# Criss-cross window attention: TensorE queues VectorE's scores before their banks are free

## The chip, the cores and the metric

The kernel runs on one core of a Trainium2 chip. The metric is device time in microseconds. One execution was also profiled: for it there is a trace of every instruction on TensorE (PE), its weight loads (PEld), VectorE (DVE), ScalarE (ACT), GpSimd (POOL) and SyncE (SP).

## The reference

An image of 224 x 224 tokens with 96 channels is projected to queries, keys and values. The first 48 channels attend within horizontal stripes of 8 rows, the other 48 within vertical stripes of 8 columns; each stripe is a window of 1792 tokens, with 28 windows in each direction. Then comes an output projection.

```python
qkv = jnp.einsum('bhwc,cd->bhwd', x, wqkv)          # x (1, 224, 224, 96), wqkv (96, 288)
scale = C2 ** (-0.5)                                # C2 = 48
qh = q[..., :C2].reshape(B * nh, sw * W, C2)        # 28 windows of 1792 tokens
ah = _softmax(jnp.einsum('bqc,bkc->bqk', qh, kh) * scale, axis=-1)
oh = jnp.einsum('bqk,bkc->bqc', ah, vh).reshape(B, H, W, C2)
...                                                 # the same over vertical stripes: ov
return jnp.einsum('bhwc,cd->bhwd', o, wo)           # o = concat(oh, ov)
```

## The kernel before

Two windows are worked at a time, so there are 28 pairs P (14 horizontal, then 14 vertical). For a pair, the scores are cut into 49 groups: for each 512 queries (the last chunk has 256) a group is 128 keys (256 keys in the last chunk) of both windows. A group G is a tile of 128 x 1024 scores in two PSUM banks; there are 28 x 49 = 1372 of them. Each has to be exponentiated and then multiplied with V (`plan_PV`, L829), which adds up in one of the banks 6 and 7 until a chunk's groups are all done. The row sums come from a column of ones in V, and the division is in the output projection.

Exponentials are the bulk of the work, and three engines share them:

- ScalarE ("a" tiles): one activation from PSUM to a buffer `PTA` (L892). Its scores go in turn to banks 0 and 1 and to banks 2 and 3. `qA` lists the tiles whose scores are queued, `actA` those whose exponential is.
- VectorE ("d" tiles): an approximation by a polynomial and the bits of the float, four passes over the 1024 columns (L911, L913, L915, L916), the last into `PTD`. The scores go to banks 4 and 5, `dps` (L898).
- GpSimd ("p" tiles): VectorE copies the scores from the same banks 4 and 5 to SBUF (L1033), and GpSimd makes six passes over them (L983 to L992), the last into `PTP`.

Scores for the last two kinds are made with one more row of the operands (KD = 50 against KA = 49), so in the trace a matmul of L198 or L724 with 50 rows is for banks 4 and 5, one with 49 rows for ScalarE.

Banks 4 and 5 hold one tile at a time. `D["cur"]` is that tile; `D["free"]` is the event after which the banks may be written again, the last pass (L916) or the copy (L1033).

The order of every engine's instructions is fixed when the program is built, by a small planner that is part of the kernel. It keeps a clock `now`, and for each engine the time at which it is free (`tfree`). `add` (L175) puts an instruction at the end of an engine's list, with a duration from the source, and gives back an event: a semaphore, its value and `vis(e)`, the planned time at which the others can see it. When an engine is free, its `pick_` function chooses what comes next; if it chooses nothing, the clock goes on to the next alarm. Afterwards `emit` (L1209) writes the lists out: an instruction whose event hasn't come waits on the semaphore, and everything behind it on its engine waits too.

`pick_pe` (L741) chooses for TensorE, in this order:

1. scores for ScalarE, when their two banks have been released by the exponential before last; else it notes in `nextfree` when that will be;
2. scores for a "p" tile, if banks 4 and 5 have none in work, fewer than NZP = 2 "p" tiles are out, and the scores fit before `nextfree`;
3. scores for a "d" tile, under the same condition on the banks;
4. one PV tile, if GRP tiles are ready (or as many as the chunk has left), or NBA - UTH of the NBA = 8 `PTA` buffers are in use, or a burst is under way and no projection is wanted;
5. a projection ("fill"): Q, K, V of the next pair or the output projection of the one before. They use the bank of 6 and 7 that PV doesn't.

If it finds nothing, `keep_warm` (L1135) may add a matmul that changes no result.

`fits` (L769) is the test of time: the work, plus 100 ns where TensorE changes between the array split in 64 x 64 tiles ("r64", for scores) and the undivided one ("r128"), may end up to `slack` ns after `nextfree`. The slack is SLACK = 160 for PV and projections, DSLACK for scores into banks 4 and 5. In planned ns, scores take 240, a PV tile 235, a pass of VectorE 1142, an exponential 917.

DUEO is read in L1120 alone, in the branch for `ORD == 0`; ORD is 1 (L90).

Of the kernel before, what the change touches and what calls it, by code (L numbers as in the profile page):

```python
# [22 lines left out]
def bass_standalone__window_attn_cswin__vision_kernel(  # L23
# [32 lines left out]
    NZP = 2  # L56
# [5 lines left out]
    SLACK = 160  # L62
    PACE = 0.5
    FDUE = 20
    DSLACK = 120
    GRP = 3
    NBA = 8
    LOOK = 7
    NPT = 400
# [5 lines left out]
    KWL = 0  # L75
    HOLD = 110
    HOLD2 = 0
    DUEO = 18
    DUES = 2.5
    DUE1 = 5  # L80
    DUEV = 20
    LATE = 10
    UTH = 2
    PSPAN = 20
    SAFE = 100
    WGAP = 170
    PADA = 5
    PADB = 1
    ENDD = 2
# [17 lines left out]
    with es:  # L107
# [60 lines left out]
        def vis(e):  # L168
            return e[2] if e is not None else 0.0
# [138 lines left out]
        def pv_bank(chg):  # L308

            if chg in pvb:  # L310
                return pvb[chg]
            return min((6, 7), key=lambda i: 1e18 if bank_free[i] == "busy" else vis(bank_free[i]))
# [368 lines left out]
        def progress():  # L681
            while lowest[0] < NGTOT and taken[lowest[0]] is not None:
                lowest[0] += 1
            return lowest[0]

        def tile_deps(G):
            P, g = divmod(G, NG)
            c = GROUPS[g][0]
            step = 512 if P == 0 else PCH
            kts = GROUPS[g][1]  # L690
            need = [(q_ready, i) for i in range((CH_Q0[c] + CH_SIZES[c] - 1) // step + 1)]
            need += [(k_ready, i) for i in range(kts[0] * 128 // step, (kts[-1] * 128 + 127) // step + 1)]
            if any((P, i) not in r for r, i in need):
                return None
            return [r[(P, i)] for r, i in need]

        def plan_QK(G, base, kk, waits):
            P, g = divmod(G, NG)
            c, kts = GROUPS[g]
            q0, qs = CH_Q0[c], CH_SIZES[c]  # L700
            b = P % 2


            def tiles(i):
                return [(64 * wdw, 64 * kh, wdw, kh) for wdw in range(2) for kh in range(2)]

            def k_ap(kt, r0, kh):
                return KT_sb[b][r0:r0 + kk, kt * 128 + 64 * kh:kt * 128 + 64 * kh + 64]

            def fn_w(e):  # L710
                for r0, c0, wdw, kh in tiles(0):
                    ins = load_weights(e, k_ap(kts[0], r0, kh), (r0, c0))
                return ins

            def fn(e):
                ins = None
                for i, kt in enumerate(kts):
                    for r0, c0, wdw, kh in tiles(i):
                        o = bank(base + wdw)[64 * kh:64 * kh + 64, i * qs:(i + 1) * qs]
                        rhs = QT_sb[b][r0:r0 + kk, q0:q0 + qs]  # L720
                        if i == 0:
                            ins = loaded_matmul(e, o, k_ap(kt, r0, kh), rhs, (r0, c0))
                        else:
                            ins = e.matmul(o, lhsT=k_ap(kt, r0, kh), rhs=rhs, start=True, stop=True)  # L724
                return ins
            ops["pe"].append((tile_deps(G), fn_w, False))
            return add("pe", waits, fn, 240.0, 425.0, "r64")
# [6 lines left out]
        D = dict(n=0, cur=None, np=0)  # L734
        P_out = []
# [5 lines left out]
        def pick_pe():  # L741
            t = now[0]

            m = len(qA)
            nextfree = None
            if progress() < NGTOT:
                G = progress()
                deps = tile_deps(G)
                if deps is not None:
                    ws = list(deps)  # L750
                    ok = True
                    if m >= 2:
                        if len(actA) <= m - 2:
                            ok = False
                        else:
                            ws.append(actA[m - 2])
                    if ok:
                        tv = max(vis(w) for w in ws)
                        if tv <= t:
                            taken[G] = "a"  # L760
                            lastA[0] = G
                            ev = plan_QK(G, 2 * (m % 2), KA, ws)
                            qA.append((G, ev))
                            return True
                        nextfree = tv

            pe_next[0] = nextfree

            def fits(occ, mode="r128", slack=SLACK):  # L769
                if mode != pe_mode[0]:  # L770
                    occ += SWITCH
                if mode != "r64":
                    occ += SWITCH
                return nextfree is None or t + occ <= nextfree + slack or nextfree - t > 1500.0

            if D["cur"] is None and len(P_out) < NZP and D["np"] < NPT and fits(240.0, "r64", DSLACK):
                lo = max(progress(), lastA[0]) + LOOKP
                for G in range(lo, min(lo + PSPAN, NGTOT - 10)):
                    deps = tile_deps(G) if taken[G] is None else None
                    ws = list(deps) + [D.get("free")] if deps is not None else [None]  # L780
                    if deps is not None and all(vis(w) <= t for w in ws):
                        taken[G] = "p"
                        D["np"] += 1
                        P_out.append(G)
                        zi = D["np"] % NZP
                        ev = plan_QK(G, 4, KD, ws)
                        D["cur"] = dict(G=G, k=0, prev=ev, qk=ev, p=zi)
                        return True
            if D["cur"] is None and fits(240.0, "r64", DSLACK):
                G = max(progress(), lastA[0]) + LOOK  # L790
                while G < NGTOT and taken[G] is not None:
                    G += 1
                if G < NGTOT - ENDD:
                    deps = tile_deps(G)
                    if deps is not None:
                        ws = list(deps) + [D.get("free")]
                        if all(vis(w) <= t for w in ws):
                            taken[G] = "d"
                            ev = plan_QK(G, 4, KD, ws)
                            D["cur"] = dict(G=G, k=0, prev=ev, qk=ev)  # L800
                            return True

            ready = []
            chg = pv_cur[0]
            if chg < NCHT:
                bi = pv_bank(chg)
                P = chg // NCH
                if (not pv_first[chg] or (bank_free[bi] != "busy" and vis(bank_free[bi]) <= t)) and P in v_ready and vis(v_ready[P]) <= t:
                    ready = [G for G in pv_left[chg] if G in pt_ev and vis(pt_ev[G][0]) <= t]
            used = sum(b is not None for b in bufA)  # L810
            f = next_fill()
            nleft = len(pv_left[chg]) if chg < NCHT else 0

            want_fill = f is not None and fits(f.occ) and not (nleft <= NRES and chg + 1 < NCHT and progress() < f.due + RDUE)
            late = want_fill and progress() > f.due - LATE and used < NBA - 1
            if ready and fits(235.0) and not late and (len(ready) >= min(GRP, nleft) or used >= NBA - UTH or not want_fill and inburst[0] > 0):
                for G in ready[:1]:
                    plan_PV(chg, G)
                inburst[0] = len(ready) - 1
                return True  # L820
            inburst[0] = 0
            if want_fill:
                f.start()
                fills_todo.remove(f)
                evac_q.append(f)
                return True
            return False
# [48 lines left out]
        def next_fill():  # L876
            for f in fills_todo:
                if f.target <= progress() and f.ready():
                    return f
            return None  # L880
# [198 lines left out]
        def early_qk(G):  # L1079
# [7 lines left out]
            qA.append((G, plan_QK(G, 2 * (G % 2), KA, tile_deps(G) + [actA[G - 2]])))  # L1087
        pad(PADA)
        early_qk(2)
# [20 lines left out]
        def refill():  # L1110

            while NXT["P"] < NP and progress() >= NXT["P"] * NG:
                P = NXT["P"]
                NXT["P"] += 1
                if P + 1 < NP:
                    pf = prep_fills(P + 1)
                    order = pf["K"] + pf["Q"][:2] + pf["V"] + pf["Q"][2:] if ORD == 0 else pf["K"] + pf["Q"] + pf["V"]
                    for i, f in enumerate(order):
                        f.target = P * NG + PACE * i
                        f.due = P * NG + NG - LOOK - DUEO + DUES * i if ORD == 0 else P * NG + (DUES * i + DUE1 if i < 8 else NG - DUEV + DUES * (i - 8))  # L1120
                        fills_todo.append(f)
# [13 lines left out]
        def keep_warm():  # L1135
# [5 lines left out]
            if tail[0] or 3000.0 - busy < WARM or t - tfree["pe"] < 60.0:  # L1141
                return False
            if pe_next[0] is not None and pe_next[0] - t < WGAP:
                return False
# [131 lines left out]
```

The softmax here doesn't subtract the row's maximum and nothing guards it: scores larger than these inputs give would overflow.

## Time and profile before

| | |
|---|---|
| time, median of 4 runs | 1082.83 us (1082.6 to 1083.24) |
| the profiled execution | 1082.6 us |
| its span, first to last instruction | 1080.8 us |
| granted TensorE clock | 0.998 |
| tiles by ScalarE, VectorE, GpSimd | 1161, 117, 94 |
| four passes of VectorE, mean of one | 1.22, 1.22, 1.21, 1.21 us |
| copy of VectorE for GpSimd, mean | 1.22 us |
| six passes of GpSimd, mean of one | 1.04, 1.89, 1.04, 2.13, 2.13, 1.05 us |

The counts are those of the lines L892, L911 and L1033 in the profile. A record of ScalarE or VectorE runs until its result is written, and overlaps the beginning of the next, so the distance from one start to the next is shorter than the mean shown. In rows of the trace, "<-" before a line names what ended the idle time of an engine.

### The profile page before, as it was taken

Reading aid. Unit: us, or ns where it says so; the run is one execution under the profiler, and the core shown is the slowest. Engines: PE = TensorE matmul, PEld = TensorE weight load, DVE = VectorE, ACT = ScalarE, POOL = GpSimd, SP = SyncE. Lnnn points to the kernel's source line nnn. Section 1 sums busy time; section 2 is a strip of 40 time slices with the busy share of each in tenths; the row PEclk is TensorE's granted clock in tenths of the full one; section 3 lists DMA queues with packets and bytes.
Section 4 is the critical chain, followed back from the end, with each engine's and each line's share of the span. In section 5 each row is a group of like instructions: output and inputs, shape, how many; then the busy total and the mean of one; then the engine's idle time right before and its main releaser. Section 6 shows DMA issues by size and latency. Waiting matters only on the chain.

```text
span 1080.8 us, 28395 instructions
## 1 busy us (share of the span) xinstructions
PE 1030.2 (95%) x12065; PEld 374.6 (35%) x12065; DVE 1026.1 (95%) x1411; ACT 1066.9 (99%) x1164; POOL 958.0 (89%) x662
## 2 busy tenths in 40 slices
PE   9999999999999999999999999999999999999997
PEld 3333333333333333333333333333333333333332
DVE  6999999999999999999999999999999999999997
ACT  7999999999999999999999999999999999999997
POOL 0499999989998999998998999999999999999995
PEclk9999999999999999999999999999999999999999
DMA  5401201110110111011111222222222222221111
GB/s 98 76 6 36 36 10 27 36 28 9 36 36 10 27 36 19 18 36 21 19 33 32 40 40 42 38 42 40 40 42 39 41 43 38 40 43 37 37 24 33
DMA packets 168999, 37.35 MB, mean 35 GB/s; under 512 B 168872, under 2 KB 168872, under 8 KB 168872
## 3 DMA queue, kind: packets, MB, share of 16 engines
q1 hardware_dynamic: 167256, 35.35, 17.6%
q8 instruction: 94, 1.54, 0.6%
q10 hardware_dynamic: 1616, 0.18, 0.1%
q14 instruction: 33, 0.27, 0.1%
HBM read 0.15 MB, written 9.63 MB: 9 GB/s over the span
## 4 chain that ended last, share of the span: by engine, by line
ACT 97%; SPq 1%; PE 0%; DMA 0%; DVE 0%; issue 0%
ACT PTA L892 97%; SPq L205 1%; DMA xT_sb<-in_x_dram 0%; PE ps L853 0%; PE ps L198 0%; DVE tmp L624 0%; DVE out_sb L647 0%; PE ps L612 0%; PE ps L1176 0%; DVE OT_sb L943 0%; PE ps L467 0%; DVE rc L618 0%; PE ps L724 0%
## 5 line engine op out<-in xcount | busy, mean ns | idle before, releaser
L892 ACT ACTIVATE PTA<-ps 128x1024 bf16<-128x1024 f32 x1161 | 1064.7, 1292 | 2.1 <-PE ps L198 2.1
L198 PE MATMUL ps<-QT_sb,KT_sb 49*64 49x512 bf16 (+3 forms) x5488 | 476.5, 364 | 43.2 <-ACT PTA L892 32.2
L853 PE MATMUL ps<-PTA,V_sb 128*64 128x512 bf16 (+1 forms) x2648 | 412.4, 365 | 0.2
L194 PEld LDWEIGHTS <-KT_sb 49*64 49x64 bf16 (+1 forms) x5488 | 138.1, 103 | 324.6 <-issue 312.6
L989 POOL TENSOR_TENSOR up_sb<-uq_sb,up_sb 128x1024 f16<-128x1024 f16 x94 | 200.1, 2128 | 7.0
L991 POOL TENSOR_TENSOR zp_sb<-zp_sb,up_sb 128x1024 f32<-128x1024 f32 x94 | 200.3, 2131 | 6.3
L853 PEld LDWEIGHTS ps<-PTA,V_sb 128*64 128x64 bf16 x2648 | 119.2, 108 | 197.7 <-issue 155.6
L985 POOL TENSOR_TENSOR uq_sb<-up_sb 128x1024 f16<-128x1024 f16 x94 | 177.9, 1892 | 7.3
L911 DVE TENSOR_SCALAR tt_sb<-ps 128x1024 f32<-128x1024 uint16 x117 | 142.9, 1221 | 11.0 <-PE ps L198 6.5
L983 POOL TENSOR_SCALAR up_sb<-zp_sb 128x1024 f16<-128x1024 uint16 x94 | 98.2, 1044 | 54.7 <-DVE zp_sb L1033 48.2
L913 DVE SCALAR_TENSOR_TENSOR sq_sb<-ps,tt_sb 128x1024 f32<-128x1024 uint16 x117 | 142.2, 1215 | 0.2
L916 DVE TENSOR_TENSOR PTD<-tt_sb,ps 128x1024 uint16<-128x1024 f32 x117 | 141.8, 1212 | 0.4
L915 DVE TENSOR_TENSOR tt_sb<-sq_sb,ps 128x1024 f32<-128x1024 f32 x117 | 141.7, 1211 | 0.1
L1033 DVE COPY zp_sb<-ps 128x1024 f32<-128x1024 f32 x94 | 115.0, 1223 | 18.4 <-PE ps L198 13.7
L647 POOL TENSOR_TENSOR out_sb<-tmp,Ph_sb 128x480 bf16<-128x480 f32 (+2 forms) x89 | 86.5, 975 | 25.4 <-DVE tmp L624 22.4
L992 POOL TENSOR_SCALAR PTP<-zp_sb 128x1024 uint16<-128x1024 f32 x94 | 98.2, 1045 | 8.2
L987 POOL TENSOR_SCALAR uq_sb<-uq_sb 128x1024 f16<-128x1024 f16 x94 | 98.2, 1044 | 8.2
L467 PE MATMUL ps<-xT_sb,w_sb 128*64 128x448 bf16 (+3 forms) x448 | 84.0, 372 | 0.8 <-DMA xT_sb<-in_x_dram 0.6
L492 DVE SCALAR_TENSOR_TENSOR KT_sb<-ksum,ps 128x448 bf16<-128x448 f32 (+1 forms) x112 | 68.8, 614 | 3.6 <-PE ps L467 2.7
L943 DVE CAST OT_sb<-ps 128x512 bf16<-128x512 f32 (+5 forms) x118 | 69.4, 592 | 1.0 <-PE ps L853 0.7
L624 DVE TENSOR_TENSOR tmp<-ps,rc 128x480 f32<-128x480 f32 (+2 forms) x92 | 53.7, 583 | 3.1
L584 DVE TENSOR_TENSOR Ph_sb<-ps,rc 128x480 bf16<-128x480 f32 x84 | 52.4, 624 | 2.9
(52 smaller groups left out, 616.5 us busy)
## 6 DMA issues: line engine op xcount, KB each, us to landing
out_dram<-out_sb SPq DMA_DIRECT2D x389, 24.0 KB, 1.9
xT_sb<-in_x_dram SPq DMA_TRANSPOSE x332, 2.6
w_sb<-in_wqkv_dram ACTq DMA_DIRECT2D x2, 54.0 KB, 3.2
out_dram<-out_sb ACTq DMA_DIRECT2D x3, 24.0 KB, 1.9
wo_sb<-in_wo_dram SPq DMA_DIRECT2D x4, 9.0 KB
wo_sb<-one_sb SPq DMA_DIRECT2D x4, 0.0 KB
```

The costliest lines, as they stand in the source:

```text
L194: return e.add_instruction(mybir.InstLdweights(tile_size=(64, 64), tile_position=pos, name=nc.get_next_instruction_name(), engine=mybir.En ...
L198: return e.add_instruction(mybir.InstMatmult(start_tensor_calc=True, stop_tensor_calc=True, tile_size=(64, 64), tile_position=pos, ldweigh ...
L853: ins = e.matmul(bk[64 * wdw:64 * wdw + 64, 0:qs], lhsT=V_sb[b][:, wdw, kt, :], rhs=pt[:, wdw * 512 + i * qs:wdw * 512 + (i + 1) * qs], st ...
L892: e = add("act", [ev, bufA_ev[sl]], lambda e, base=base, sl=sl: e.activation(PTA[sl][:], ps[:, base * 512:(base + 2) * 512], ACTF.Exp, sca ...
L911: return lambda e: e.tensor_scalar(tt_sb[:], frac, (HA + RT) * U, CD / U ** 3, ALU.add, ALU.mult)
L913: return lambda e: e.scalar_tensor_tensor(sq_sb[:], frac, (HA - RT) * U, tt_sb[:], ALU.add, ALU.mult)
L915: return lambda e: e.tensor_tensor(tt_sb[:], sq_sb[:], frac, ALU.mult)
L916: return lambda e: e.tensor_tensor(PTD[sl][:].bitcast(U16), tt_sb[:], dps, ALU.add)
L985: return e.tensor_tensor(q, u, u, ALU.mult)
L989: return e.tensor_tensor(u, q, u, ALU.mult)
L991: return e.tensor_tensor(z, z, u, ALU.add)
L1033: ev = add("dve", [d["prev"], zp_rd[zi]], lambda e: e.tensor_copy(zp_sb[zi][:], dps), D_OCC[0], D_OCC[0] + 107.0)
```

## The change

Planner constants and three conditions in `pick_pe` are changed. A tile for banks 4 and 5 may now be chosen when its inputs and the release of the banks are at most QE = 300 ns in the future, instead of being visible at the planner's present. The wait on the semaphore then stands at the head of TensorE's list, and in `fits` the time until the release is added to the duration. DSLACK goes from 120 to 200, GRP from 3 to 2, UTH from 2 to 4, DUEO from 18 to 25.

```diff
-    DSLACK = 120
-    GRP = 3
+    DSLACK = 200
+    GRP = 2
...
-    DUEO = 18
+    DUEO = 25
...
-    UTH = 2
+    UTH = 4
...
+    QE = 300
...
-            if D["cur"] is None and len(P_out) < NZP and D["np"] < NPT and fits(240.0, "r64", DSLACK):
+            if D["cur"] is None and len(P_out) < NZP and D["np"] < NPT and fits(240.0 + max(0.0, vis(D.get("free")) - t), "r64", DSLACK):
...
-                    if deps is not None and all(vis(w) <= t for w in ws):
+                    if deps is not None and all(vis(w) <= t + QE for w in ws):
                         taken[G] = "p"
...
-            if D["cur"] is None and fits(240.0, "r64", DSLACK):
+            if D["cur"] is None and fits(240.0 + max(0.0, vis(D.get("free")) - t), "r64", DSLACK):
...
-                        if all(vis(w) <= t for w in ws):
+                        if all(vis(w) <= t + QE for w in ws):
                             taken[G] = "d"
```

## The prediction

> **What bounds the kernel now.** I read the page's share of engines first, then the chain of waits, then the view of who waited for whom, the instructions of single lines, and a timeline around one late tile.
>
> ```profile
> PE 1030.2 (95%) x12065; PEld 374.6 (35%) x12065; DVE 1026.1 (95%) x1411; ACT 1066.9 (99%) x1164; POOL 958.0 (89%) x662
> ...
> L892 ACT ACTIVATE PTA<-ps 128x1024 bf16<-128x1024 f32 x1161 | 1064.7, 1292 | 2.1 <-PE ps L198 2.1
> ```
>
> ```profile
> 20.34 1050.61 ACT PTA L892 x1146
> ```
>
> ScalarE is the bound. The second fence is a piece of the chain of waits: from 20.34 us on, 1146 exponentials follow each other in 1050.61 us, 0.9168 us each, with nothing between them. So the time is a start of 20 us, an end of some 7 us, and 0.917 us for every tile left to ScalarE. The 1372 tiles of scores are split 1161 to ScalarE, 117 to VectorE (four passes each, L911 to L916) and 94 to GpSimd after a VectorE copy (L1033). The change gains what it moves off ScalarE, tile by tile; nothing else in steady state can shorten the kernel.
>
> Could the others take more? Here is the stretch 20 to 1060 us (busy us and instructions of each engine), and who waited for whom:
>
> ```profile
> 20.00:1060.00 1040.00, 997.39 (x11755) 362.23 (x11756) 1001.24 (x1353) 1039.83 (x1136) 947.90 (x644) 1.00 0.18 33
> ```
>
> ```profile
> POOL up_sb L983 <- DVE zp_sb L1033: 48.2, 6, 38.5
> ...
> PE ps L198 <- ACT PTA L892: 32.2, 91, 0.5
> ...
> DVE zp_sb L1033 <- PE ps L198: 13.7, 38, 0.7
> ...
> DVE tt_sb L911 <- PE ps L198: 6.5, 20, 0.7
> ...
> DVE tt_sb L911 <- PE ps L724: 2.4, 8, 0.6
> ...
> DVE zp_sb L1033 <- PE ps L724: 1.8, 7, 0.4
> ```
>
> VectorE idles 38.8 us of that stretch (1040 less 1001.2). The last three rows, with the row of 13.7, sum to 24.4 us of VectorE waiting for the scores of its own next tile: this is what the change is aimed at. GpSimd's 48.2 us is mostly one wait of 38.5 before its first tile; the other five sum to 9.7.
>
> One such wait, in the timeline (start, duration, engine, line):
>
> ```profile
> 383.65 1.21 DVE L916 TENSOR_TENSOR PTD<-tt_sb,ps 128x1024 uint16<-128x1024 f32 x1
> ...
> 384.77 0.55 DVE L435 CAST V_sb<-ps 128x384 bf16<-128x384 f32 x1
> 384.81 0.62 PE L853 MATMUL ps<-PTA,V_sb 128*64 128x512 bf16 x4
> ...
> 385.61 0.38 PE L198 MATMUL ps<-QT_sb,KT_sb 50*64 50x512 bf16 x4
> ...
> 386.03 1.22 DVE L1033 COPY zp_sb<-ps 128x1024 f32<-128x1024 f32 x1 [0.71 <-PE ps L198]
> ```
>
> L916 ends at 384.86 and the banks are free. TensorE has just taken two PV tiles (0.62 us), then owes ScalarE its scores, and issues VectorE's (the 50-row matmul) at 385.61, 0.75 us after the release; VectorE stood still for 0.71. Pairing each release (end of L916 or L1033) with the next 50-row scores over the whole trace gives 0.31 us on average and 0.05 at the least, for 211 tiles.
>
> **The change, part by part.** *QE = 300.* The planner may now queue VectorE's scores when their banks will be free within 0.3 us, where it had to see them free. TensorE then does nothing until the release. In the example it would not take the PV pair but wait from 384.75 or so to 384.91 (release plus 0.05), run 0.38, and VectorE would begin near 385.34, just after its cast ends at 385.32: the 0.71 is gone. It doesn't help where ScalarE's own scores are due: by the source a start of VectorE's scores in the last 0.14 us before that (0.24 + 0.10 + wait, against a slack of 0.20), or during their 0.24 us, must wait. That is 0.38 of each 0.917 us, in which the wait is 0.19 us on average, so 0.08 us over all; today's excess over the floor is 0.31 - 0.05 = 0.26. I take it that two thirds of the excess goes, and two thirds of the 24.4 us with it: 16.3 us. Bounds: 0 (other work of VectorE fills the place anyway, as in the 76 of 209 tiles that began with no idle time before them) and 24.4; a loss is a rival below.
>
> What VectorE time is worth: from one pass to the next start is 1.12 us (383.65 to 384.77), so a VectorE tile costs 4 x 1.12 = 4.5 us, and a tile moved also makes the kernel 0.917 us shorter, in which VectorE would have worked too. 16.3 us buy 16.3 / (4.5 + 0.92) = 3.0 tiles. GpSimd: two thirds of its 9.7 us is 6.5; its six passes for a tile take 98.2 + 177.9 + 98.2 + 200.1 + 200.3 + 98.2 = 872.9 us for 94 tiles, 9.3 each, some 9.8 with the gaps: 0.6 tile more, each with a VectorE copy of 1.12, so VectorE's share falls to (16.3 - 0.6 x 2.0) / 5.4 = 2.8. Sum: 3.4 tiles off ScalarE, 3.1 us.
>
> *DSLACK 120 to 200.* VectorE's scores may push ScalarE's by 0.08 us more. What absorbs that is in ScalarE's own records:
>
> ```profile
> L892 ACT ACTIVATE PTA<-ps x1114: 1068/1322/1359, 29.4 to 1049.5; 128x1024 bf16<-128x1024 f32 x186
> ```
>
> Their starts move, their ends don't: the ends stand 0.91 to 0.92 us apart for every tile after 20 us, while the duration runs from 1.07 to 1.36. An early tile waits inside its record; a late one is short. The whole run's minimum is 1.02, so the cushion is 1.36 - 1.02 = 0.34, of which at worst 0.29 is used. Another 0.08 costs 0.03 at the few worst places: 0.1 us. Without the cushion it would be 211 x 0.08 = 17 us.
>
> *TensorE's waiting.* Behind the held scores stand all of its queue: ScalarE's next scores, PV, projections. The holds reach 0.3 us, 0.12 on average if TensorE comes free at a random point of its 0.24 us jobs: 211 x 0.12 = 25 us. It is paid from TensorE's idle time in the stretch, 1040 - 997.4 = 42.6 us, and so costs nothing; its cover ends at 42.6 / 211 = 0.20 us for a mean hold. The Trainium skill (Perfetto Trace Analysis, Identifying the Most-Contended Engine) says that busy time of pipelined matmuls is no measure of how full TensorE is, and the share of weight loads is: here 35%, not 95%; by that the cover would be several times larger and even full holds would cost nothing. On the other side the skill (TensorE: Matmul & The Clock Gate, Step-by-step) has matmuls stay in program order, only weight loads being pulled ahead; by that alone every hold delays ScalarE's scores behind it, and 25 us would be the loss if ScalarE had no cushion. I go by the 42.6 us.
>
> *GRP 3 to 2, UTH 2 to 4.* PV starts with two tiles ready instead of three, or four buffers in use instead of six. Between ScalarE's scores at 0.917 us a burst of three doesn't fit today either (a single PV tile shows as 0.41 us, a pair as 0.62). I cost it at 0, hidden by the same 42.6 us; splitting a pair costs 0.41 x 2 - 0.62 = 0.20, and of some 1372 / 2 pairs a third could be split: 46 us, as much as the cover, so this is its upper bound, and its lower is a few us of earlier projections, which no row prices; I take 0, the nearest row being today's pairs. *DUEO* is read only where ORD is 0; ORD is 1, so it does nothing. No DMA is added; the output transfers wait for L647 on GpSimd as before.
>
> *Sum.* -3.1 + 0.1 = -3.0 us. The profiled run took 1082.6 us, of which 1080.8 is the span; the median is 1082.83, 0.2 more. So 1079.8, with a span near 1077.8.
>
> **Rivals.** *More is gained:* all 29.4 us idle before L1033 and L911 (18.4 + 11.0) go, and GpSimd begins earlier (its first wait of 38.5 us is four of its tiles long; half of it would be two). 29.4 / 5.4 = 5.4, plus 2: 7 tiles, 6.5 us, 1076.3. For it: the durations in the planner's source (1.14 a pass) agree with the rows, so the plan is kept on chip. Against: ScalarE's scores come first.
>
> *The idle time only changes place:* VectorE's place is taken by projections that come earlier or later, and the tile counts stay within one or two: 1082.8 less 0 to 1.8, say 1082. For it: VectorE's last 38.8 us hold 11 to 14 us that have nothing to do with scores, and a tile is a large piece.
>
> *TensorE runs out (slower):* holds above 0.20 us on average, or more switching between PV and scores, use up the 42.6 us; then PV falls behind, the eight PTA buffers fill, and ScalarE, at 0 idle now, waits. With full holds 211 x 0.3 = 63 us, 63 - 42.6 = 20 us, half of it on ScalarE as its cushion takes single waits: 10 us, 1093. For it: TensorE's 95%; L198 already waits 32.2 us at the head in 91 places. Against: those waits cost ScalarE nothing.
>
> **Chances.** Forecast (gain of 1.8 to 4.2 us) 0.50; more 0.20; no shift 0.15; slower 0.15. A measurement of this kernel can tell 0.2% (2.2 us) from no change, so faster begins at 1080.7 and slower at 1085.0. Of the forecast 0.40 lies beyond that and 0.10 within; "more" is all faster; the second rival is within; of the slower, 0.13 is over 1085.0. That makes faster 0.60, same 0.27, slower 0.13. The forecast's own range is 1078.6 to 1081.0; to leave no more than 2 in 10 out I go from 1075.2, below the 1076.3 of the first rival, to 1084.6, where only the slower case is outside.
>
> **What would show it.** Right: L892 x1157 or 1158, L911 x119 to 121, L1033 x94 or 95; the rows of VectorE waiting for L198 and L724 at 8 us, not 24; the piece of the chain still 0.917 us a tile; shorter minimum of L892 (near 1.02) with no idle time before it. A new wait of PE L198 for L916 or L1033, near 25 us, is the hold. Wrong: L892 x1161 or more; idle time before L892 beyond the first 20 us; L853 late and the exponentials waiting for PTA buffers.

## The result, and the profile after

| | before | after |
|---|---|---|
| median | 1082.83 us (57 runs) | 1081.11 us (37 runs) |
| ratio, with its 95% interval | | 0.9984 (0.998 to 0.9989) |
| the profiled execution, its span | 1082.6, 1080.8 us | 1081.15, 1079.3 us |
| tiles by ScalarE, VectorE, GpSimd | 1161, 117, 94 | 1159, 119, 94 |

The change made the kernel 1.7 us faster, 0.16%. One execution of the experiment e9_slack500_no_qe below took 2700.49 us where its other ten took 1081.61 to 1082.53; its ratio leaves that one out, and as it is the one that was profiled, nothing is read from a trace of e9. In the changed kernel's text every line stands one further down than before (L892 is now L893). First the page's groups after the change (busy us, mean ns of one, then the idle time before them):

```profile
L893 ACT ACTIVATE PTA<-ps 128x1024 bf16<-128x1024 f32 x1159 | 1062.9, 1289 | 2.1 <-PE ps L199 2.1
...
L912 DVE TENSOR_SCALAR tt_sb<-ps 128x1024 f32<-128x1024 uint16 x119 | 145.3, 1221 | 11.4 <-PE ps L199 8.2
...
L1034 DVE COPY zp_sb<-ps 128x1024 f32<-128x1024 f32 x94 | 114.7, 1221 | 8.7 <-PE ps L199 5.9
```

and the piece of the chain of waits that is the kernel's body:

```profile
20.57 1048.78 ACT PTA L893 x1144
```

1048.78 / 1144 is 0.9168 us a tile, as before. Two tiles have gone from ScalarE to VectorE, 2 x 0.917 = 1.8 us, and that is all of the gain. The stretch from 20 to 1060 us shows what paid for them (PE, PEld, DVE, ACT, POOL busy), and the view of waits where it came from (total us, times, longest):

```profile
20.00:1060.00 1040.00, 1001.21 (x11792) 361.62 (x11794) 1010.75 (x1362) 1039.76 (x1136) 948.51 (x644) 1.00 0.17 33
```

```profile
POOL up_sb L984 <- DVE zp_sb L1034: 48.5, 7, 38.2
...
DVE tt_sb L912 <- PE ps L199: 8.2, 23, 1.0
...
DVE zp_sb L1034 <- PE ps L199: 5.9, 20, 0.5
...
DVE tt_sb L912 <- PE ps L725: 1.2, 5, 0.5
...
DVE zp_sb L1034 <- PE ps L725: 0.8, 3, 0.3
```

VectorE works 9.5 us longer in that stretch (1010.75 against 1001.24), and two tiles of four passes at 1.12 are 9.0. Its waits for its own scores are 16.1 us instead of 24.4. GpSimd's waits are what they were.

A held tile in the timeline of the changed kernel (start, duration, engine, line, idle time before):

```profile
62.29 1.21 DVE L917 TENSOR_TENSOR PTD<-tt_sb,ps 128x1024 uint16<-128x1024 f32 x1
...
62.90 0.38 PE L199 MATMUL ps<-QT_sb,KT_sb 49*64 49x512 bf16 x4
...
63.41 0.68 DVE L944 CAST OT_sb<-ps 128x512 bf16<-128x512 f32 x1
63.55 0.27 PE L199 MATMUL ps<-QT_sb,KT_sb 50*64 50x256 bf16 x4 [0.27 <-DVE PTD L917]
...
64.02 1.21 DVE L1034 COPY zp_sb<-ps 128x1024 f32<-128x1024 f32 x1
```

TensorE stands at the 50-row scores from 63.28, the last pass ends at 63.50, the scores start 0.05 us later, and the copy follows the cast at 64.02 with no idle time. That is the change doing what it says. How often it does is the point of the experiments.

### The profile page after: what moved, and what is told of

It reads as the page before. It is cut to its first block, busy times and chain, and to the rows that moved or that the text cites. A ratio compares the mean times of both kernels' runs of the same rounds, so it can differ in the third digit from the quotient of the medians.

```text
span 1079.3 us, 28436 instructions
## 1 busy us (share of the span) xinstructions
PE 1031.8 (96%) x12081; PEld 373.1 (35%) x12081; DVE 1034.8 (96%) x1420; ACT 1065.0 (99%) x1162; POOL 957.4 (89%) x661
## 4 chain that ended last, share of the span: by engine, by line
ACT 97%; SPq 1%; PE 0%; DVE 0%; DMA 0%; issue 0%
ACT PTA L893 97%; SPq L206 1%; DMA xT_sb<-in_x_dram 0%; PE ps L854 0%; DVE tmp L625 0%; PE ps L199 0%; DVE out_sb L648 0%; PE ps L613 0%; DVE rc L619 0%; DVE OT_sb L944 0%; PE ps L468 0%; PE ps L725 0%; PE ps L1177 0%
## 5 line engine op out<-in xcount | busy, mean ns | idle before, releaser
L893 ACT ACTIVATE PTA<-ps 128x1024 bf16<-128x1024 f32 x1159 | 1062.9, 1289 | 2.1 <-PE ps L199 2.1
L854 PE MATMUL ps<-PTA,V_sb 128*64 128x512 bf16 (+1 forms) x2652 | 410.9, 364 | 0.4 <-DVE QT_sb L504 0.2
L854 PEld LDWEIGHTS ps<-PTA,V_sb 128*64 128x64 bf16 x2652 | 119.2, 108 | 195.8 <-issue 152.2
L912 DVE TENSOR_SCALAR tt_sb<-ps 128x1024 f32<-128x1024 uint16 x119 | 145.3, 1221 | 11.4 <-PE ps L199 8.2
L984 POOL TENSOR_SCALAR up_sb<-zp_sb 128x1024 f16<-128x1024 uint16 x94 | 98.2, 1044 | 54.6 <-DVE zp_sb L1034 48.5
L917 DVE TENSOR_TENSOR PTD<-tt_sb,ps 128x1024 uint16<-128x1024 f32 x119 | 144.3, 1212 | 0.6
L914 DVE SCALAR_TENSOR_TENSOR sq_sb<-ps,tt_sb 128x1024 f32<-128x1024 uint16 x119 | 144.7, 1216 | 0.2
L916 DVE TENSOR_TENSOR tt_sb<-sq_sb,ps 128x1024 f32<-128x1024 f32 x119 | 144.2, 1212 | 0.3
L1034 DVE COPY zp_sb<-ps 128x1024 f32<-128x1024 f32 x94 | 114.7, 1221 | 8.7 <-PE ps L199 5.9
```

Of the source, the lines that this page charges most:

```text
L854: ins = e.matmul(bk[64 * wdw:64 * wdw + 64, 0:qs], lhsT=V_sb[b][:, wdw, kt, :], rhs=pt[:, wdw * 512 + i * qs:wdw * 512 + (i + 1) * qs], st ...
L893: e = add("act", [ev, bufA_ev[sl]], lambda e, base=base, sl=sl: e.activation(PTA[sl][:], ps[:, base * 512:(base + 2) * 512], ACTF.Exp, sca ...
L912: return lambda e: e.tensor_scalar(tt_sb[:], frac, (HA + RT) * U, CD / U ** 3, ALU.add, ALU.mult)
L914: return lambda e: e.scalar_tensor_tensor(sq_sb[:], frac, (HA - RT) * U, tt_sb[:], ALU.add, ALU.mult)
L916: return lambda e: e.tensor_tensor(tt_sb[:], sq_sb[:], frac, ALU.mult)
L917: return lambda e: e.tensor_tensor(PTD[sl][:].bitcast(U16), tt_sb[:], dps, ALU.add)
```

## The experiments

The theory under test: time follows the number of tiles left to ScalarE at 0.917 us each; the look-ahead raises VectorE's share only as far as `fits` lets its scores in ahead of ScalarE's; and a late score of ScalarE costs nothing until a cushion in ScalarE's own records is used up. The rivals: the gain comes from the other constants; waiting at the head of the queue costs TensorE, and through it ScalarE, what VectorE gains; or a late score is a late exponential.

**One part at a time.** The first three kernels take the change apart.

```diff
 # e1_qe_alone: QE = 300 kept
-    DSLACK = 200
-    GRP = 2
-    UTH = 4
+    DSLACK = 120
+    GRP = 3
+    UTH = 2
```

> QE = 300 with the old DSLACK 120, GRP 3 and UTH 2. The program has 1161 ScalarE tiles, 118 VectorE, 93 GpSimd. Theory (time follows the number of ScalarE tiles at 0.917 us each, the look-ahead pays only where the slack lets it in): the time of before, 1082.8, within 0.5 us; VectorE's wait for its own scores stays above 20 us. Rival (the look-ahead itself is the gain): the changed kernel's 1081.1, with that wait near 16 us.

```diff
 # e2_retune_alone
-    QE = 300
+    QE = 0
```

> DSLACK 200, GRP 2 and UTH 4, but QE = 0, so scores for banks 4 and 5 are queued only when the banks are free. The program has 1161, 117 and 94 tiles, as before the change. Theory: 1082.8 to 1083.1 (one planned wait of ScalarE of 0.25 us). Rival (the gain is from taking PV earlier, or from the slack): 1081.1 to 1082.

```diff
 # e3_qe_dslack: QE = 300 and DSLACK = 200 kept
-    GRP = 2
-    UTH = 4
+    GRP = 3
+    UTH = 2
```

> QE = 300 and DSLACK 200, with the old GRP 3 and UTH 2. The program has 1160, 119 and 93 tiles. Theory: one tile less than before, 1081.9, plus at most 0.35 us that the plan has ScalarE wait once: 1081.9 to 1082.3. Rival (GRP and UTH cost or gain nothing): 1081.1.

Measured, as ratios to runs of the kernel before on the same chip (its median there 1082.48 us):

| | median, us | ratio (95%) | tiles | VectorE's wait for its scores |
|---|---|---|---|---|
| e1_qe_alone | 1084.14 | 1.0024 (1.0013 to 1.0035) | 1161, 118, 93 | 22.0 us |
| e2_retune_alone | 1083.07 | 1.0005 (0.9996 to 1.0014) | 1161, 117, 94 | 25.7 us |
| e3_qe_dslack | 1081.81 | 0.9996 (0.9987 to 1.0004) | 1160, 119, 93 | 14.7 us |

(The wait is the sum of the four rows shown for the changed kernel. e1 and e3 also have DUEO at 18, which nothing reads here.) Neither half gains anything alone. The constants without the look-ahead leave the tiles and the time as they were. Look-ahead and slack together, e3, cut the wait as far as the whole change does, and its median is 0.7 us below that of before, though its interval still holds 1. So the look-ahead needs the slack; GRP and UTH add the last tile. The expectation for e1 missed: it has 1161 tiles, but 1.7 us more time. Its windows around one place say why (busy us of PE, PEld, DVE, ACT, POOL; then the granted clock):

```profile
160.00:165.00 5.00, 4.82 (x86) 2.66 (x82) 4.97 (x6) 5.00 (x7) 4.83 (x3) 1.00 0.02 5
165.00:170.00 5.00, 3.43 (x48) 1.18 (x44) 4.82 (x8) 5.00 (x7) 4.67 (x5) 0.95 0.01 2
170.00:173.00 3.00, 3.00 (x28) 0.96 (x24) 2.22 (x4) 2.56 (x3) 2.83 (x3) 0.50 0.50 104
173.00:176.00 3.00, 3.00 (x28) 0.91 (x28) 1.87 (x4) 1.97 (x2) 2.92 (x2) 0.50 0.28 53
```

From 165 to 170 TensorE is busy 3.43 of 5 us; from 170 to 176 its clock is at half, scores take 0.63 us instead of 0.38, and ScalarE, until then never idle, works 4.5 of 6 us. A second such place is at 361 us. In the trace of the kernel before, no slice of 5 us between 20 and 1060 has TensorE busy for less than 4.22 us; in e1 the two thinnest have 3.43 and 3.83, and they are the ones ahead of the two places. The Trainium skill (TensorE: Matmul & The Clock Gate, Part 1) has a gate that halves the clock after an idle window of about 3.4 us. Here TensorE was thinly loaded and not idle, with no gap over 0.54 us, and the clock fell all the same; the measurement decides. Over the 11 runs of e1 the time goes with the mean granted clock: 1081.81 at 1.000, 1083.4 to 1084.1 at 0.997 or 0.998, 1088.66 at 0.991. So the extra time isn't the held scores' doing as such: the order that comes of them leaves two thin stretches. Whether that is so was tried.

**Filling the thin stretches.** WGAP is the planner's limit for the matmuls that only keep TensorE busy.

```diff
 # e8_qe_wgap, against e1_qe_alone
-    WGAP = 170
+    WGAP = 120
```

> QE alone as in e1_qe_alone, with WGAP 120 in place of 170, which lets TensorE do more of its matmuls that change no result; the program again has 1161, 118 and 93 tiles, but in its plan no stretch of 3.4 us leaves TensorE under half busy, where e1_qe_alone has two under 0.42. Theory (e1_qe_alone lost its time to two stretches of half clock): 1082.3 to 1083, a granted clock of 0.998 or more, no idle time of ScalarE after 20 us and runs within 1 us of each other. Rival (the loss comes from the look-ahead's waits at the head of the queue): 1084 again.

1082.27 us, ratio 0.9997 (0.9988 to 1.0006), all 11 runs between 1081.85 and 1082.68, granted clock 0.999 or more. The windows of the same place:

```profile
165.00:170.00 5.00, 4.68 (x74) 1.94 (x70) 4.80 (x7) 5.00 (x7) 4.66 (x5) 1.00 0.39 79
170.00:173.00 3.00, 2.99 (x30) 0.80 (x28) 2.84 (x6) 3.00 (x5) 2.84 (x3) 1.00 0.46 97
```

TensorE is busy 4.68 of the 5 us, the clock stays at 1.00, and ScalarE doesn't stop. The same 1161 tiles and the same look-ahead (33 of VectorE's scores start within 0.06 us of the release in both), without the half clock, take the time of before. The rival, that the waits at the head cost 1.7 us, falls.

**GRP by itself.**

```diff
 # e4_grp3, against the changed kernel
-    GRP = 2
+    GRP = 3
```

> The changed kernel with GRP 3 in place of 2. The program has 1162, 122 and 88 tiles. Theory of tiles alone, ScalarE never waiting: 1081.1 + 3 x 0.917 = 1083.9. Rival (TensorE's order becomes the bound, PV or projections fall behind): the plan has ScalarE wait 7.2 us in six places, three of 2 us or more, so 1091 and idle time before the exponentials of 5 us or more.

1093.83 us (four runs), ratio 1.0107 (1.0094 to 1.0121): the rival's case, and worse. Who kept ScalarE waiting:

```profile
ACT PTA L893 <- PE ps L854: 5.6, 3, 2.7
ACT PTA L893 <- PE ps L199: 4.6, 7, 1.2
```

and one of the three places in its timeline:

```profile
285.41 0.55 DVE L436 CAST V_sb<-ps 128x384 bf16<-128x384 f32 x1
...
286.01 0.64 PE L854 MATMUL ps<-PTD,V_sb 128*64 128x512 bf16 x2 [0.76 <-DVE V_sb L436]
...
287.12 1.02 ACT L893 ACTIVATE PTA<-ps 128x1024 bf16<-128x1024 f32 x1 [2.72 <-PE ps L854]
```

The PV tiles of the next pair need its V (L436 writes it). V is late, TensorE stands 0.76 us at the first PV tile for it, and ScalarE, with no PTA buffer free, has waited 2.72 us when L854 gives one back. The theory of tiles counts only where ScalarE doesn't wait, and here it does: three tiles more than the changed kernel are 2.8 us, and ScalarE's idle time before its exponentials is 10.2 us instead of 2.1, together 10.9 of the 11.0 us between the two profiled executions (1092.14 and 1081.15). Here too the clock was halved at two places (285 and 442 us). At the first, ScalarE stops at 284.40 and scores at 284.45 still take 0.38 us, so its wait began before the half clock. Why GRP of 3 with UTH of 4 makes V late while 3 with 2 (e3) doesn't was not tried; that the pair of constants decides it is shown, by 12.0 us between e4 and e3 on the same chip.

**How far may ScalarE's scores be pushed?** Two kernels go on from the changed one.

```diff
 # e5_dslack500
-    DSLACK = 200
+    DSLACK = 500
 # e6_slacks
-    SLACK = 160
-    DSLACK = 200
+    SLACK = 260
+    DSLACK = 240
```

> The changed kernel with DSLACK 500 in place of 200: VectorE's scores may push ScalarE's by 0.5 us. The program has 1155 ScalarE tiles, 122 VectorE and 95 GpSimd; the planner itself counts on 14.6 us of waiting by ScalarE in some 96 places. Theory (ScalarE's records hold a cushion of 0.34 us that the planner doesn't know, so waits below that vanish): 1081.1 - 4 x 0.917 = 1077.4 plus what exceeds 0.34 us, at most 3 us: 1077.5 to 1080.5. Rival (no cushion, a late score is a late exponential): 1077.4 + 14 = 1091.

> The changed kernel with DSLACK 240 and SLACK 260 (PV and projections may also push ScalarE's scores, by 0.1 us more). The program has 1156, 120 and 96 tiles; the planner counts on 9.6 us of ScalarE's waiting, no single one in steady state over 0.13 us. Theory (cushion): 1081.1 - 3 x 0.917 = 1078.4, no idle time before the exponentials after the start, shorter minimum of their durations. Rival (no cushion): 1088.

e5 took 1079.36 us, ratio 0.9979 (0.9963 to 0.9994), with one of nine runs at 1086.49, its clock at 0.990; e6 1079.42, ratio 0.997 (0.9959 to 0.9982), where the kernel before had 1082.64. The planners counted on 14.6 and 9.6 us of waiting by ScalarE; the chip showed some 2.4 and 1.5 after the first 30 us. e6 missed its expectation of 1078.4 by 1.0 us; the theory had counted on no such loss, and 1.5 us covers it. The exponentials of e5 from 30 to 1050 us (count, then min/median/max ns):

```profile
L893 ACT ACTIVATE PTA<-ps x1112: 1017/1183/1358, 28.9 to 1049.7; 128x1024 bf16<-128x1024 f32 x186
```

and three long pieces of the chain of waits that are ScalarE's:

```profile
299.32 158.86 ACT PTA L893 x173
460.08 113.78 ACT PTA L893 x124
...
702.81 280.90 ACT PTA L893 x306
```

The median record is 1.18 us instead of 1.32, as low as 1.017 and never lower: the cushion is used to its floor. The pieces still run at 0.918 us a tile, and where the floor is touched the chain breaks, between 458 and 460 us for instance. Pairing each exponential with the start of its scores: as long as these started within 0.37 us of the release of their banks, the ends stayed 0.92 us apart; 39 tiles were later and lost 2.4 us together. In e6 37 tiles after 30 us were later and lost 1.5. The difference is one tile's 0.9 us, which is why e5, with 1155 tiles, takes what e6 takes with 1156.

e5 also shows what limits the look-ahead. VectorE's scores that started at once, less than 0.06 us after the release: 9 of 210 before the change, 43 of 212 after it, 142 of 216 in e5; the mean delay 0.31, 0.23 and 0.09 us; VectorE's wait 24.4, 16.1 and 5.7 us.

**A version built on this.** The planner is told of the cushion, so that it doesn't count on waits that don't happen, and its slacks are widened; LOOK, NRES, DUE1, UTH and WGAP go with it so that no stretch is thin.

```diff
 # e7_cushion_plan, against the changed kernel
-            return add("pe", waits, fn, 240.0, 425.0, "r64")
+            return add("pe", waits, fn, 240.0, 225.0 if kk == KA else 425.0, "r64")
-    SLACK = 160
-    DSLACK = 200
+    SLACK = 200
+    DSLACK = 280
...
+    LOOK = 6
+    NRES = 1
+    DUE1 = 7
+    UTH = 2
+    WGAP = 120
```

> The planner is told of the cushion: scores for ScalarE count as done 0.225 us after their start instead of 0.425, and DSLACK 280, SLACK 200, LOOK 6, NRES 1, DUE1 7, UTH 2, WGAP 120. The program has 1157, 120 and 95 tiles and no planned wait of ScalarE. Theory (tiles times 0.917): two tiles fewer than the changed kernel, 1081.1 - 1.8 = 1079.3, with VectorE's wait for its own scores near 10 us. Rival (TensorE's order gives it back: late scores beyond 0.34 us or a lower clock): 1081 or more.

1078.65 us, ratio 0.9962 (0.995 to 0.9975), five runs from 1077.85 to 1079.33: the fastest here, 4 us below the kernel before. Its groups and its piece of the chain:

```profile
L893 ACT ACTIVATE PTA<-ps 128x1024 bf16<-128x1024 f32 x1157 | 1061.1, 1269 | 1.9 <-PE ps L199 1.9
...
L912 DVE TENSOR_SCALAR tt_sb<-ps 128x1024 f32<-128x1024 uint16 x120 | 146.5, 1221 | 9.1 <-PE ps L199 6.2
```

```profile
14.54 1053.52 ACT PTA L893 x1149
```

1053.52 / 1149 is 0.9169. VectorE's wait is 11.5 us. The unbroken piece begins at 14.54 and not at 20.57, where the changed kernel still has a short wait of ScalarE, some 0.3 us; that is a part of the 0.65 us by which this kernel beats the expectation.

**Is the look-ahead still needed there?** Both fast versions without it:

```diff
 # e9_slack500_no_qe, against e5_dslack500
 # e10_cushion_no_qe, against e7_cushion_plan
-    QE = 300
+    QE = 0
```

> e5_dslack500 with QE = 0: the wide slack without the look-ahead. The program has 1160, 118 and 94 tiles, against 1155, 122 and 95. Theory (look-ahead and slack only pay together): from the 1079.4 of e5_dslack500, five tiles more are 4.6 us, less the 2.2 us that ScalarE lost there to scores later than its cushion, which may be less here: 1081.5 to 1084. Rival (the slack alone is the gain): 1079.5 or less.

> e7_cushion_plan with QE = 0. The program has 1161, 117 and 94 tiles, against 1157, 120 and 95. Theory: from the 1078.65 of e7_cushion_plan, four tiles more at 0.917 us: 1082.3, within 0.6. Rival (the other constants carry the gain): 1079.5 or less.

1082.08 us, ratio 0.9995 (0.9986 to 1.0004), and 1082.70, ratio 1.0003 (0.9994 to 1.0012). The kernel before took 1082.52 on that chip. Without the look-ahead the wide slacks are worth nothing that clears the noise: the two kernels are 2.7 and 4.05 us slower than with it, and the intervals of their ratios to the kernel before hold 1.

## Why the prediction was right, and where its size was off

The change gained, and the time lies within the stated range of 1075.2 to 1084.6, but it gained 1.7 us where 3.0 were forecast. The 1081.11 is 0.1 us outside the forecast's own stretch, and above the 1080.7 at which the prediction let "faster" begin: that is its "same", which had 0.27 against 0.60. Of its signs, 119 and 94 tiles for VectorE and GpSimd, 0.917 us a tile and a shorter minimum of the exponentials came; ScalarE kept 1159 tiles and not 1157 or 1158, and VectorE's wait stayed at 16.1 us and not 8.

*What bounds the kernel, and what a tile is worth*: right. ScalarE's exponentials follow each other at 0.917 us before and after. 2 tiles are 1.8 us, the medians differ by 1.7.

*QE = 300, "two thirds of the excess goes"*: the mechanism was right, and this term was mis-sized. 16.3 us of VectorE's wait was to go and 8.3 went, one third; the mean delay fell from 0.31 to 0.23, not to 0.13. I took the part of the 0.917 us in which ScalarE's scores bar the way, 0.38, for the only obstacle, so that 59% of the tiles would start at once. 43 of 212 did. The test in `fits` bars more than that as long as DSLACK is 200: with 500 alone changed (e5) it is 142 of 216.

*What VectorE time is worth*: right, as far as whole tiles can tell. VectorE's idle time in the stretch fell by 9.5 us, 8.3 of it the wait; at 4.5 + 0.92 a tile that is 1.75, and it became two. The 0.6 tile for GpSimd was too much and did not come: its waits for L1034 after the first were 9.7 us and are 10.3 (48.5 - 38.2).

*DSLACK's cost, 0.1 us for a cushion of 0.34*: right, and it was nothing. The records between 30 and 1050 us reach lower than before (1034 ns for 1068) while the ends stay 0.92 us apart:

```profile
L893 ACT ACTIVATE PTA<-ps x1114: 1034/1318/1358, 29.6 to 1049.8; 128x1024 bf16<-128x1024 f32 x186
```

e5 found the cushion's end close to where it was placed: scores up to 0.37 us after the release cost nothing, and the 0.05 of an immediate start plus 0.34 is 0.39.

*TensorE's waiting, 25 us covered by 42.6*: it costs nothing, as said, but it was much smaller: the idle time before the 43 held scores sums to 1.1 us in the trace, of which the view of waits has two:

```profile
PE ps L199 <- DVE PTD L917: 0.4, 2, 0.3
```

So the wait near 25 us, named as a sign, did not come: 29 of the 43 show no idle time at all, so TensorE mostly came free about when the banks did. In e5 the 142 have 11.4 us before them, still inside the cover. The rule on weight loads and the row on idle time were both safe here, so this doesn't tell them apart.

*GRP and UTH at 0*: right as a sum, wrong in kind. They bring no time of their own (e2), but at the new order the two have to fit each other: with UTH 4, GRP 3 makes V late and costs some 12 us (e4), while GRP 3 with UTH 2 does not (e3). The rival "TensorE runs out" was thus real, by another way than the one I priced: not the length of the holds, but thin or blocked stretches. *DUEO* wasn't tried by itself; nothing in the source reads it here.

*The rivals*: "more is gained" needs a wider slack than the change has, and then comes to 4.0 us (e7) and not 6.5. "The idle time only changes place" was priced at 0 to 1.8 us, so the 1.7 alone would fit it as well; against it stands that VectorE's idle time in the stretch did fall, by 9.5 of 38.8 us. With each half of the change alone most of VectorE's wait stays (e1, e2), and the tiles with it.

## What to carry to other kernels

Where one engine is saturated, count the pieces of work it still has, and price every change by that count; a wait elsewhere is worth only the whole tiles that its time can buy. An instruction that may be queued early still has to pass the test that protects the bottleneck: open the two together, and measure the bottleneck's true slack from the spread of its records before choosing the margin. And look at the clock in the windows after reordering TensorE, since an order with the same work can lose 2 us to one thin stretch (2.3 at the first place of e1).

## What the runs showed of the hardware

ScalarE's record of the same activation lasts from 1.02 to 1.36 us while the ends stay 0.92 us apart; starts can slip by 0.34 us without any loss of rate, and an engine that shows no idle time and the same rate may be using up that cushion. Scores up to 0.37 us after the release of their banks cost nothing in e5. The TensorE clock fell to 0.50 for 6 us after a stretch with 3.43 of 5 us busy and no gap over 0.54; of the 11 executions of the same program one kept a mean clock of 1.000. So the spread of the runs (1081.81 to 1088.66 us in e1, 1081.85 to 1082.68 in e8) was itself a sign.
